# Attention kernel: the transposes of the norm and of the memory's writes in two halves of 64 rows, moved within their slots

## The chip, the cores and the metric

The kernel runs on one core of one Trainium2 chip. The time is the device time of one execution in microseconds (us), read as the median of several runs. The core has a matrix engine (PE; its loading of the stationary operand is listed apart as PEld), a vector engine (DVE), a scalar engine (ACT), a general engine (POOL), and queues that start transfers (SP and others). Each engine works through its own instructions strictly in the order in which they were recorded, and waits on the others by semaphores. Matmuls write to PSUM, which holds eight banks of 128 partitions x 512 float32. ACT and DVE read the results from there.

## The reference, cut to what matters

Four layers, A, B, A, B, each with a layer norm in front and a residual sum behind. A is a linear attention with a learned feature map, B is an attention over four segments of 512 tokens with a memory that is carried from segment to segment:

```python
x = x + A(layernorm(x)); x = x + B(layernorm(x))      # and both once more
# B, 32 heads of 16 columns, N = 4 segments of L = 512 tokens, g = sigmoid(beta) per head
for s in range(N):
    qs, ks, vs = q[:, :, s], k[:, :, s], v[:, :, s]
    p = softmax(qs @ ks.T * Dh**-0.5 + causal_mask)
    a_dot = p @ vs
    a_mem = (phi(qs) @ M) / (phi(qs) @ z + 1e-6)       # phi(t) = t + 1 if t > 0 else exp(t)
    out = g * a_mem + (1 - g) * a_dot
    M, z = M + phi(ks).T @ vs, z + phi(ks).sum()
```

## The kernel before

Everything is float32; products that need the full precision are made of three products of a rounded part and its remainder ("hi" and "lo", hh and hl for the normalised x). The method `steps` of `LayerB` records the attention as one row of **slots**. A segment has eight units m (four groups of eight heads, two halves each), and a unit has five slots, so a slot is named m.j, with 0.0 to 7.4 in each segment. In a slot stand, in this order on PE: the logits of the slot (two matmuls side by side into the tile `lg`, two banks, one buffer), the products from which the row maxima of a later unit are taken ("maxima"), whatever the table names with a leading "<", in slots m.0 the reads of the memory and the weighted sums of the previous unit (`weighted`), and last the quarters of projections that the table names without "<" (Q, V, O).

Four tables (FIRST for the first segment, GAPS for the two in the middle, and LAST and FINAL for the last one of each of the two B layers) say what stands in each slot. The words that matter here: `<t0` to `<t3` transpose the features phi(k) of one group for the memory's write, and `m0` to `m3` are the product and the update that follow; `<ln` is one step of the norm for the next segment, and four of these steps per segment transpose the four 128-token tiles of x (`columns`); `<turn` transposes what the A layer left (in a first segment only), `<max` puts finished maxima into place, `<a0` to `<a3` read the memory. The wrapper `Ordered` and the function `held` keep ACT, DVE, POOL, SP and PE in the order of the recording.

A transpose is a matmul with the identity. `tp` makes one of a block of 128 x 128, with all 128 rows of the array; four of them fill one PSUM tile. Logits, maxima and the projections in the slots use the array in two halves of 64 rows: two matmuls with `tile_position` 0 and 64 run side by side, each into a bank of its own. Reads and `weighted` use column strips instead (128 x 32).

The eight banks are four buffers `g`, two for `lg`, one each for `mx` and `my`. The maxima of a slot take the pair mx, my in slots m.0, m.1 and m.3, and two `g` in m.2 and m.4 (SPARE). A pair of projections holds two `g` for two to four slots. DVE reads each bank of maxima with custom instructions ("tops", each followed by a short READ_ACCUMULATOR). For a write, ACT copies the transposed features from PSUM to the tile KN. For the norm, ACT copies the transposed x to hh and then DVE subtracts, from the same bank, to hl; I call this the subtraction below.

Of the kernel before, what the change touches and what calls it, by code (L numbers as in the profile page):

```python
# [7 lines left out]
F32 = mybir.dt.float32  # L8
# [46 lines left out]


FIRST = """
0.0 <max v3 | 0.1 Q2/6              | 0.2 Q2/6          | 0.3 Q2/6 | 0.4 Q2/6
1.0 <t0 <turn <max m0 | 1.1 fin Q3/6 | 1.2 Q3/6         | 1.3 Q3/6 | 1.4 Q3/6
2.0 <ln <t1 <turn <max m1 | 2.1 fin O/6 | 2.2 O/6       | 2.3 O/6 | 2.4 O/6  # L60
3.0 <ln <turn <turn <max | 3.1 fin O/6 | 3.2 O/6        | 3.3 O/6 | 3.4 O/6
4.0 <ln <ln <max | 4.1 fin Q0+/6    | 4.2 Q0+/6 cv0     | 4.3 Q0+/6 cv1 | 4.4 load Q0+/6
5.0 <t2 <max m2 | 5.1 fin V+/6      | 5.2 V+/6 n        | 5.3 V+/6 n | 5.4 V+/6 w
6.0 <t3 <max m3 | 6.1 fin Q1+/6     | 6.2 Q1+/6 n       | 6.3 Q1+/6 n cv2 | 6.4 Q1+/6 w
7.0 <max <a0+ | 7.1 fin V+/6 w      | 7.2 V+/6 n        | 7.3 V+/6 n | 7.4 V+/6 w
"""
# [35 lines left out]
def interleave_kernel(ctx, tc, x_in, a_wqkv, a_wphi, a_wo, b_wq, b_wk, b_wv, b_wo, b_beta,  # L102
                      c_ident, c_mask, c_bd, out):
    nc = tc.nc
    MUL, ADD, SUB, MAX, MIN = ALU.mult, ALU.add, ALU.subtract, ALU.max, ALU.min
# [17 lines left out]
    def PS(tag, bufs, shape=(P, 512)):  # L123
        return ps.tile(list(shape), F32, tag=tag, bufs=bufs, name=nm(tag))
# [54 lines left out]
    def tp(*a):  # L179
        work[0] += 108  # L180
        return held(nc.tensor.transpose(*a))  # L181
# [831 lines left out]
    class LayerB:  # L1013
# [409 lines left out]
        def steps(self, side, after, table_end):  # L1423
# [3 lines left out]
            N = 8 * NSEG  # L1427
# [6 lines left out]
            outs, turns, proj = {}, {}, {}  # L1434
# [153 lines left out]
    for i in range(2):  # L1588
# [3 lines left out]
        a2 = la[i].pass2()  # L1592
# [40 lines left out]
```

## Time and profile before

| | |
|---|---|
| median of 3 runs | 1307.09 us (1305.85 to 1308.08) |
| the profiled execution | 1307.07 us, span 1305.4 us |
| PE busy | 1266.3 us, 97% of the span |
| DVE busy | 1073.8 us, 82% |
| ACT busy | 835.9 us, 64% |
| POOL busy | 757.8 us, 58% |
| granted PE clock | 0.999 |

The span is that of the instructions in one profiled execution; 1.7 us of its time lie around it. The two B layers' slots lie at about 280 to 660 us and 916 to 1300 us of the span. Rows of a timeline give the start, the duration, the engine, the line, the operation and what it writes and reads, and in brackets how long the engine stood idle before and who released it. A matmul's duration is longer than its share of the engine, since matmuls overlap: the distance of starts is what counts.

### The profile page before, as it was taken

The numbers are of one execution on the slowest core, as the hardware profiler recorded it, in microseconds if no ns is written. First come the engines' busy times: TensorE is split into PE (matmuls) and PEld (weight loads), VectorE is DVE, ScalarE is ACT, GpSimd is POOL, SyncE is SP. The second block draws the span as 40 slices with busy tenths as digits, with TensorE's granted clock in tenths as the row PEclk, the third lists the DMA queues.
The fourth block names the chain that finished last, engine by engine and source line by source line (L and its number), as shares of the span: only waits on it lengthen the run. The fifth ranks groups of instructions, "written<-read, shape, count | busy, mean of one in ns | idle before, by whom it ended". The sixth has DMA issues, their size and how long they took to land.

```text
span 1305.4 us, 41985 instructions
## 1 busy us (share of the span) xinstructions
PE 1266.3 (97%) x16488; PEld 988.1 (76%) x16488; DVE 1073.8 (82%) x3499; ACT 835.9 (64%) x1214; POOL 757.8 (58%) x1124
## 2 busy tenths in 40 slices
PE   7999989999999999999999999999999999999987
PEld 6887868877777777777768887787777777778765
DVE  4776868798998998998867767797899899898995
ACT  5556444648778788777644434455678878877754
POOL 2568855425657768667324346562356766767653
PEclk9999999999999999999999999999999999999999
DMA  6387358545655545545451101855646555554432
GB/s 213 106 314 258 123 175 254 175 125 147 185 164 152 160 126 142 160 134 162 128 174 54 66 34 37 290 176 162 163 127 205 163 141 143 144 142 113 120 84 82
DMA packets 134420, 196.59 MB, mean 151 GB/s; under 512 B 15440, under 2 KB 61648, under 8 KB 133456
## 3 DMA queue, kind: packets, MB, share of 16 engines
q1 hardware_dynamic: 133408, 193.80, 49.1%
q8 instruction: 131, 2.15, 0.7%
q14 instruction: 65, 0.53, 0.1%
q10 hardware_dynamic: 816, 0.11, 0.1%
HBM read 101.05 MB, written 39.85 MB: 108 GB/s over the span
## 4 chain that ended last, share of the span: by engine, by line
PE 77%; DVE 15%; issue 2%; ACT 2%; POOL 2%; DMA 2%; SPq 0%; DVEq 0%; ACTq 0%; POOLq 0%
PE g L177 60%; PE lg L177 6%; PE g L181 4%; PE mx L177 3%; DVE g L155 3%; DVE U L155 2%; PE lg L181 2%; DVE mx L155 2%; DVE my L155 2%; DVE es L155 1%; PE my L177 1%; POOL P L155 1%; DVE mxs L155 1%; ACT P L155 1%; DMA P<-in 1%
## 5 line engine op out<-in xcount | busy, mean ns | idle before, releaser
L155 ACT ACTIVATE P<-lg 128x1024 f32<-128x1024 f32 x316 | 324.1, 1026 | 94.8 <-PE lg L177 75.8
L155 POOL TENSOR_SCALAR_AFFINE_SELECT P<-P 128x256 f32<-128x256 f32 (+1 forms) x448 | 190.0, 442 | 227.4 <-ACT P L155 205.7
L155 DVE CUSTOM_DVE_ANT_0 g<-g,mask 128x128 f32<-128x128 f32 (+3 forms) x392 | 189.4, 538 | 7.0 <-PE g L177 6.7
L155 DVE CUSTOM_DVE_ANT_0 mx<-mx,mask 128x512 f32<-128x512 f32 (+2 forms) x316 | 158.8, 503 | 38.9 <-PE my L177 28.7
L177 PE MATMUL g<-hh,wqk 64*128 64x512 f32 (+1 forms) x960 | 183.2, 393 | 0.7 <-SPq L155 0.4
L177 PE MATMUL g<-w,oh 64*128 64x512 f32 (+2 forms) x848 | 161.8, 380 | 2.6 <-ACT oh L155 2.6
L155 DVE CUSTOM_DVE_ANT_0 my<-my,mask 128x512 f32<-128x512 f32 (+2 forms) x316 | 163.5, 517 | 0.0
L177 PE MATMUL lg<-e,e 64*128 64x512 f32 (+1 forms) x1010 | 145.8, 343 | 7.6 <-ACT P L155 7.5
L177 PE MATMUL g<-P,v 128*32 128x128 f32 (+3 forms) x2064 | 151.7, 433 | 0.2
L177 PE MATMUL g<-w,hh 64*128 64x512 f32 (+1 forms) x672 | 143.5, 395 | 2.4 <-ACT w L155 1.3
L155 DVE DVE_READ_ACCUMULATOR2_ANT mxs<- 128x1 f32 x1024 | 142.9, 140 | 0.0
L177 PEld LDWEIGHTS lg<-e,e 64*128 64x128 f32 x1010 | 92.7, 185 | 51.7 <-ACT P L155 19.7
L177 PEld LDWEIGHTS g<-hh,wqk 64*128 64x128 f32 (+1 forms) x960 | 100.0, 185 | 19.5 <-SPq L155 2.0
L177 PEld LDWEIGHTS g<-P,v 128*32 128x32 f32 x2064 | 65.5, 109 | 60.8 <-issue 53.6
L177 PEld LDWEIGHTS g<-w,oh 64*128 64x128 f32 (+1 forms) x848 | 94.7, 187 | 18.8 <-ACT oh L155 3.5
L155 ACT COPY tb<-g 128x512 f32<-128x512 f32 (+1 forms) x132 | 71.1, 575 | 52.3 <-PE g L177 52.0
L177 PE MATMUL g<-w,ol 64*128 64x512 f32 (+2 forms) x424 | 101.0, 377 | 1.9 <-DVE ol L155 1.9
L177 PE MATMUL g<-hl,wqk 64*128 64x512 f32 (+1 forms) x480 | 102.1, 390 | 0.0
L177 PEld LDWEIGHTS g<-w,hh 64*128 64x128 f32 (+1 forms) x672 | 83.8, 188 | 17.9 <-ACT w L155 1.6
L177 PE MATMUL g<-w,hl 64*128 64x512 f32 (+1 forms) x336 | 89.3, 392 | 0.0
L155 POOL TENSOR_TENSOR ta<-tb,ta 128x512 fp32r<-128x512 f32 x60 | 76.2, 1291 | 14.0 <-ACT ta L155 11.1
L177 PE MATMUL mx<-e,e 63*128 63x256 f32 (+3 forms) x323 | 82.0, 318 | 0.8 <-DVE r L155 0.8
(163 smaller groups left out, 2935.7 us busy)
## 6 DMA issues: line engine op xcount, KB each, us to landing
e<-ta SPq DMA_DIRECT2D x384, 128.0 KB
wqk<-wqk SPq DMA_DIRECT2D x128, 256.0 KB
x<-x SPq DMA_DIRECT2D x48, 256.0 KB
pq<-tb SPq DMA_DIRECT2D x24, 256.0 KB
tb<-pq SPq DMA_DIRECT2D x24, 256.0 KB
x<-xr SPq DMA_DIRECT2D x22, 256.0 KB
xr<-x SPq DMA_DIRECT2D x20, 256.0 KB
x<-in SPq DMA_DIRECT2D x16, 256.0 KB
```

The lines of the kernel that those rows point to most:

```text
L155: i = f(*a, **k)
L177: return held(nc.tensor.matmul(*a, **k))
L181: return held(nc.tensor.transpose(*a))
```

## The change

Three things change, all of them in the B layers' slots only (`banks` is set there and nowhere else).

The new `tp_halves` transposes a block of 128 tokens by 128 columns as two matmuls of 64 rows, with `tile_position` 0 and 64, each into its own bank, 64 columns wide. `columns` and `writes` use it there: four blocks give eight small matmuls in place of four large ones, into two banks in place of one. What was one ACT copy of 512 columns is now two of 256, and the one DVE subtraction of 512 columns is now two of 256.

The new method `pair` chooses the two banks: mx and my in slots m.2 and m.4, where the maxima use `g`, and two buffers `g` in the other slots.

In the tables, the transposes leave the slots m.0. `<t0` to `<t3` go from 1.0, 2.0, 5.0 and 6.0 to 0.4, 1.4, 4.4 and 5.4. The four `<ln` that transpose go from 2.0, 3.0, 4.0 and 4.0 to 2.4, 3.2, 3.3 and 3.4. In a slot m.j with j > 0 they are recorded behind the slot's maxima and ahead of its projections. There are 28 groups of four blocks from `columns` and 24 from `writes` in the slots, 52 in all, spread over seven segments (the last segment of the second B layer has none). The transposes of `<turn`, those of the A layers and those ahead of the slots stay as they were.

```diff
 GAPS = """
-3.0 <ln <turn <turn <max <a2 | 3.1 fin O/6 | 3.2 O/6    | 3.3 O/6 | 3.4 O/6
-4.0 <ln <ln <max <a2 | 4.1 fin Q0+/6 | 4.2 Q0+/6 cv0    | 4.3 Q0+/6 cv1 | 4.4 load begin Q0+/6
+3.0 <turn <turn <max <a2 | 3.1 fin O/6 | 3.2 <ln O/6    | 3.3 <ln O/6 | 3.4 <ln O/6
+4.0  <max <a2 | 4.1 fin Q0+/6 | 4.2 Q0+/6 cv0    | 4.3 Q0+/6 cv1 | 4.4 <t2 load begin Q0+/6
...
+    def tp_halves(outs, in_):
+
+        work[0] += 60
+        for row, out in zip((0, 64), outs):
+            held(nc.tensor.transpose(out, in_[row : row + 64], ident[row : row + 64, row : row + 64],
+                                     tile_position=(row, 0)))
...
+    banks = [None]
+
     def columns(hT, t, x):
+        if banks[0] is not None:
+            pts = [pt[:, 0 : NC * 64] for pt in banks[0]()]
+            for kc in range(NC):
+                tp_halves([pt[:, kc * 64 : (kc + 1) * 64] for pt in pts], x[:, kc * P : (kc + 1) * P])
+            views = [[h[:, :, t * P + 64 * r : t * P + 64 * r + 64] for h in hT]
+                     + [pts[r].rearrange("p (k t) -> p k t", k=NC)] for r in range(2)]
+            for hv, _, pv in views:
+                act.copy(hv, pv)
+            for hv, lv, pv in views:
+                dve.tensor_tensor(out=lv, in0=pv, in1=hv.bitcast(F32), op=SUB)
+            return
         pt = PS("g", G)
...
             ph = self.st[s, c]["phi", 1]
-            pt = PS("g", G)
+            pts = [pt[:, 0 : 4 * 64] for pt in self.pair()]
             for t in range(4):
-                tp(pt[:, t * P : (t + 1) * P], ph[:, t * P : (t + 1) * P], ident)
+                tp_halves([pt[:, t * 64 : (t + 1) * 64] for pt in pts], ph[:, t * P : (t + 1) * P])
             pk = T2("KN", 1)
-            act.copy(pk, pt)
+            for r in range(2):
+                act.copy(pk.rearrange("p (t r f) -> p r t f", t=4, r=2)[:, r],
+                         pts[r].rearrange("p (t f) -> p t f", t=4))
...
+        def pair(self):
+
+            return [PS(t, 1) for t in ("mx", "my")] if self.k % R in SPARE else [PS("g", G) for _ in range(2)]
...
+                banks[0] = self.pair if 0 <= k < R * N else None
```

**PE, slot 4.0 of the third segment of the first B layer.** Before, from the logits (lg) over the maxima (mx, my) to the memory's reads (mem). x are tiles of normalised tokens, w and oh or ol a projection's operands.

```order
L177 MATMUL g_8325<-w_4999,ol_7641 128x512
L177 MATMUL lg_8438<-e_433_2751,e_434_2752 128x512 x2
L177 MATMUL mx_8442<-e_453_2833,e_452_2832 128x256
L177 MATMUL my_8443<-e_453_2833,e_452_2832 128x256
L177 MATMUL mx_8442<-e_453_2833,e_452_2832 128x384
L177 MATMUL my_8443<-e_453_2833,e_452_2832 128x384
L181 MATMUL g_8452<-ident,x_6675 128x128 x4
L181 MATMUL g_8459<-ident,x_6677 128x128 x4
L177 MATMUL g_8471<-mem_2746,tb_1298_7678 32x34 x32
```

And the same place in the changed kernel:

```order
L177 MATMUL g_8441<-w_5058,ol_7745 128x512
L177 MATMUL lg_8596<-e_433_2751,e_434_2752 128x512 x2
L177 MATMUL mx_8600<-e_453_2833,e_452_2832 128x256
L177 MATMUL my_8601<-e_453_2833,e_452_2832 128x256
L177 MATMUL mx_8600<-e_453_2833,e_452_2832 128x384
L177 MATMUL my_8601<-e_453_2833,e_452_2832 128x384
L177 MATMUL g_8615<-mem_2746,tb_1317_7795 32x34 x32
```

The two groups of transposes between the maxima and the reads are gone from this slot; one went to slot 3.3 and one to 3.4.

**PE, slot 3.2 of the same segment, the changed kernel**, from the maxima (here in two `g`) to the first matmul of the projection O (pair w, oh):

```order
L177 MATMUL g_8464<-e_434_2752,e_433_2751 128x384
L177 MATMUL g_8465<-e_434_2752,e_433_2751 128x384
L187 MATMUL mx_8477<-ident,x_6778 128x64
L187 MATMUL my_8478<-ident,x_6778 128x64
L187 MATMUL mx_8477<-ident,x_6778 128x64
L187 MATMUL my_8478<-ident,x_6778 128x64
L187 MATMUL mx_8477<-ident,x_6778 128x64
L187 MATMUL my_8478<-ident,x_6778 128x64
L187 MATMUL mx_8477<-ident,x_6778 128x64
L187 MATMUL my_8478<-ident,x_6778 128x64
L177 MATMUL g_8441<-w_5058,oh_6699 128x512
```

Before, the projection followed the maxima directly; the eight half transposes now stand between them and write mx and my, which the maxima of slot 3.3 write next.

**DVE, slots 3.2 and 3.3 there.** Before, from the last top of slot 3.2 (g) through the four of slot 3.3 (mx, my) to the first of slot 3.4 (ISA are a top and its READ_ACCUMULATOR, mxs the maxima):

```order
L155 ISA g_8349,mxs_2748<-g_8349,mask 128x384
L155 ISA mxs_2748 128x1
L155 ISA mx_8382,mxs_2748<-mx_8382,mask 128x256
L155 ISA mxs_2748 128x1
L155 ISA my_8383,mxs_2748<-my_8383,mask 128x256
L155 ISA mxs_2748 128x1
L155 ISA mx_8382,mxs_2748<-mx_8382,mask 128x256
L155 ISA mxs_2748 128x1
L155 ISA my_8383,mxs_2748<-my_8383,mask 128x256
L155 ISA mxs_2748 128x1
L155 ISA g_8414,mxs_2748<-g_8414,mask 128x512
```

And in the changed kernel, from the same top on:

```order
L155 ISA g_8465,mxs_2748<-g_8465,mask 128x384
L155 ISA mxs_2748 128x1
L155 TENSOR_TENSOR hl_8303<-mx_8477,hh_8302 128x4x64
L155 TENSOR_TENSOR hl_8303<-my_8478,hh_8302 128x4x64
L155 ISA mx_8512,mxs_2748<-mx_8512,mask 128x256
L155 ISA mxs_2748 128x1
L155 ISA my_8513,mxs_2748<-my_8513,mask 128x256
L155 ISA mxs_2748 128x1
L155 ISA mx_8512,mxs_2748<-mx_8512,mask 128x256
L155 ISA mxs_2748 128x1
L155 ISA my_8513,mxs_2748<-my_8513,mask 128x256
L155 ISA mxs_2748 128x1
```

Two subtractions of half the width now stand ahead of the tops of slot 3.3 (two more follow those, and two follow the tops of 3.4); before, DVE had none from 3.1 to 3.4, and two of the full width in 4.0.

More of the change, by code (lines that the diff above doesn't have):

```diff
@@ L57 @@
 FIRST = """
[L58 to L64, printed above, removed]
+0.0 <max v3 | 0.1 Q2/6              | 0.2 Q2/6          | 0.3 Q2/6 | 0.4 <t0 Q2/6
+1.0 <turn <max m0 | 1.1 fin Q3/6 | 1.2 Q3/6         | 1.3 Q3/6 | 1.4 <t1 Q3/6
+2.0 <turn <max m1 | 2.1 fin O/6 | 2.2 O/6       | 2.3 O/6 | 2.4 <ln O/6
+3.0 <turn <turn <max | 3.1 fin O/6 | 3.2 <ln O/6        | 3.3 <ln O/6 | 3.4 <ln O/6
+4.0  <max | 4.1 fin Q0+/6    | 4.2 Q0+/6 cv0     | 4.3 Q0+/6 cv1 | 4.4 <t2 load Q0+/6
+5.0 <max m2 | 5.1 fin V+/6      | 5.2 V+/6 n        | 5.3 V+/6 n | 5.4 <t3 V+/6 w
+6.0 <max m3 | 6.1 fin Q1+/6     | 6.2 Q1+/6 n       | 6.3 Q1+/6 n cv2 | 6.4 Q1+/6 w
 7.0 <max <a0+ | 7.1 fin V+/6 w      | 7.2 V+/6 n        | 7.3 V+/6 n | 7.4 V+/6 w
@@ L67 @@
 GAPS = """
-0.0 <max <a0 n | 0.1 fin Q2/6 n     | 0.2 Q2/6 n        | 0.3 Q2/6 n cv3 | 0.4 Q2/6
-1.0 <t0 <turn <max <a1 m0 | 1.1 fin Q3/6 | 1.2 Q3/6     | 1.3 Q3/6 | 1.4 Q3/6
-2.0 <ln <t1 <turn <max <a1 m1 | 2.1 fin O/6 | 2.2 O/6   | 2.3 O/6 | 2.4 O/6
-3.0 <ln <turn <turn <max <a2 | 3.1 fin O/6 | 3.2 O/6    | 3.3 O/6 | 3.4 O/6
-4.0 <ln <ln <max <a2 | 4.1 fin Q0+/6 | 4.2 Q0+/6 cv0    | 4.3 Q0+/6 cv1 | 4.4 load begin Q0+/6
-5.0 <t2 <max <a3 m2 | 5.1 fin V+/6 | 5.2 V+/6 n N       | 5.3 V+/6 n N | 5.4 V+/6
-6.0 <t3 <max <a3 m3 | 6.1 fin Q1+/6 | 6.2 Q1+/6 n N     | 6.3 Q1+/6 n N cv2 | 6.4 Q1+/6
+0.0 <max <a0 n | 0.1 fin Q2/6 n     | 0.2 Q2/6 n        | 0.3 Q2/6 n cv3 | 0.4 <t0 Q2/6
+1.0 <turn <max <a1 m0 | 1.1 fin Q3/6 | 1.2 Q3/6     | 1.3 Q3/6 | 1.4 <t1 Q3/6
+2.0 <turn <max <a1 m1 | 2.1 fin O/6 | 2.2 O/6   | 2.3 O/6 | 2.4 <ln O/6
+3.0 <turn <turn <max <a2 | 3.1 fin O/6 | 3.2 <ln O/6    | 3.3 <ln O/6 | 3.4 <ln O/6
+4.0  <max <a2 | 4.1 fin Q0+/6 | 4.2 Q0+/6 cv0    | 4.3 Q0+/6 cv1 | 4.4 <t2 load begin Q0+/6
+5.0 <max <a3 m2 | 5.1 fin V+/6 | 5.2 V+/6 n N       | 5.3 V+/6 n N | 5.4 <t3 V+/6
+6.0 <max <a3 m3 | 6.1 fin Q1+/6 | 6.2 Q1+/6 n N     | 6.3 Q1+/6 n N cv2 | 6.4 Q1+/6
 7.0 <max <a0+ | 7.1 fin V+/6      | 7.2 V+/6 n N        | 7.3 V+/6 n N | 7.4 V+/6
@@ L79 @@
 1.0 <turn <max <a1 | 1.1 fin Q3/6   | 1.2 Q3/6          | 1.3 Q3/6 | 1.4 Q3/6
-2.0 <ln <turn <max <a1 | 2.1 fin O/6 | 2.2 O/6          | 2.3 O/6 | 2.4 O/6
-3.0 <ln <turn <turn <max <a2 | 3.1 fin O/6 | 3.2 O/6    | 3.3 O/6 | 3.4 O/6
-4.0 <ln <ln <max <a2 | 4.1 fin v/2  | 4.2 v/2 cv0       | 4.3 v/2 cv1 | 4.4 v/2
+2.0 <turn <max <a1 | 2.1 fin O/6 | 2.2 O/6          | 2.3 O/6 | 2.4 <ln O/6
+3.0 <turn <turn <max <a2 | 3.1 fin O/6 | 3.2 <ln O/6    | 3.3 <ln O/6 | 3.4 <ln O/6
+4.0  <max <a2 | 4.1 fin v/2  | 4.2 v/2 cv0       | 4.3 v/2 cv1 | 4.4 v/2
 5.0 <max <a3 | 5.1 fin v/2          | 5.2 v/2           | 5.3 v/2 | 5.4 v/2
@@ L1554, in steps @@
                         do(w, s, k)
-            put_off[0] = None
+            put_off[0], banks[0] = None, None
             for f in self.late + self.rows:
```

## The prediction

> **What bounds the kernel now.** I read the page first, then busy time by windows, then the chain of waits inside the slots, then timelines of PE and DVE at each place where a transpose leaves or arrives.
>
> ```profile
> span 1305.4 us, 41985 instructions
> PE 1266.3 (97%) x16488; PEld 988.1 (76%) x16488; DVE 1073.8 (82%) x3499; ACT 835.9 (64%) x1214; POOL 757.8 (58%) x1124
> PE 77%; DVE 15%; issue 2%; ACT 2%; POOL 2%; DMA 2%; SPq 0%; DVEq 0%; ACTq 0%; POOLq 0%
> ```
>
> PE carries 77% of the chain, DVE 15%. For the unit from slot 3.1 to 4.1 of the third segment (first B layer) the window gives, after the window and its length, PE, PEld and DVE busy:
>
> ```profile
> 515.79:528.13 12.34, 12.34 (x188) 9.69 (x185) 11.34 (x44) 7.76 (x10) 6.29 (x10) 1.00 0.40 110
> ```
>
> DVE is busy 11.34 of 12.34 us. So in the slots two engines are nearly full, and the chain confirms it; in the unit after this one it lies on DVE for 8 us, from here to the next row of PE:
>
> ```profile
> 528.92 0.69 DVE mx L155
> ...
> 536.77 0.66 PE g L181 x4
> ```
>
> Within a unit DVE falls behind PE from m.1 to m.4, where tops come fast, and catches up in m.0, where PE spends most of its time on `weighted`. The change takes work off PE in m.0 and puts work on DVE, and two banks, into m.2 to m.4. That is where I expect its price.
>
> **What is removed from PE.** Timeline of PE: the last pair of maxima, then transposes, then the reads of the memory: slot 3.0 with one group, slot 4.0 with two, and a slot without any.
>
> ```profile
> 512.03 0.34 PE L177 MATMUL mx<-e,e 63*128 63x384 f32 x1
> ...
> 512.89 0.77 PE L177 MATMUL g<-mem,tb 128*32 128x34 f32 x64
> ```
> ```profile
> 523.91 0.34 PE L177 MATMUL mx<-e,e 63*128 63x384 f32 x1
> ...
> 524.18 1.09 PE L181 MATMUL g<-ident,x 128*128 128x128 f32 x8
> 525.20 0.77 PE L177 MATMUL g<-mem,tb 128*32 128x34 f32 x64
> ```
> ```profile
> 572.59 0.33 PE L177 MATMUL my<-e,e 63*128 63x384 f32 x1
> 572.86 0.77 PE L177 MATMUL g<-mem,tb 128*32 128x34 f32 x64
> ```
>
> Starts lie 0.86, 1.29 and 0.27 us apart. So one group alone costs 0.86 - 0.27 = 0.59 us, two cost 1.02, the second 0.43. The first includes the step into the full array and out again. In a first segment, slots 1.0 to 3.0 keep `<turn` transposes, and there each group saves only 0.43.
>
> Per middle segment: four single slots (1.0, 3.0, 5.0, 6.0) and two with two groups (2.0, 4.0), 4 x 0.59 + 2 x 1.02 = 4.4 us; per first segment about 3.9; in the last segment of the first layer (2.0, 3.0, 4.0) 2.2. All: 4 x 4.4 + 2 x 3.9 + 2.2 = 27.6 us.
>
> **What is added to PE.** 52 groups of four pairs of half transposes. No row shows one.
>
> ```profile
> L181 PE MATMUL g<-ident,x 128*128 128x128 f32 x256 | 38.0, 277 | 1.1 <-ACT x L155 1.1
> ...
> L181 PEld LDWEIGHTS g<-ident,x 128*128 128x128 f32 x256 | 29.5, 140 | 9.6 <-issue 3.1 <-ACT x L155 1.3 <-DVE mxs L155 1.0
> ```
> ```profile
> L177 PEld LDWEIGHTS mx<-e,e 63*128 63x128 f32 x316 | 57.0, 186 | 8.8 <-issue 2.4 <-DVE r L155 1.3 <-DVE mxs L155 0.7
> ```
>
> A full transpose takes 0.43 / 4 = 0.11 us. If the two halves of a pair run side by side, as 64-row matmuls do (mx and my below start 0.01 apart), and half the moving columns take half the time, a pair costs 0.06, a group 0.24. If the pair is as slow as a full block, 0.11 and 0.43. Below 0.24 I see no row, and nothing negative is possible for instructions that must issue. I take 0.24, because loading for a transpose lasts 140 ns against 186 for other matmuls, which says that the load is not what fills the 0.11. Sum 52 x 0.24 = 12.5 us. PE alone would therefore gain 27.6 - 12.5 = 15.1 us. No full-array step is added: neighbours in m.1 to m.4 use 64 rows already.
>
> **What is added to DVE and ACT.**
>
> ```profile
> L155 DVE TENSOR_TENSOR hl<-g,hh 128x512 fp32r<-128x512 f32 x48 | 32.1, 686 | 8.6 <-ACT hh L155 8.4
> ...
> L155 DVE TENSOR_TENSOR ot<-g,r 128x256 f32<-128x256 f32 x64 | 27.2, 425 | 2.2
> ```
> ```profile
> L155 ACT COPY tb<-g x132: 358/587/630, 46.4 to 1274.5; 128x512 f32<-128x512 f32 x124, 128x256 f32<-128x256 f32 x8
> ```
>
> A half subtraction lasts 0.42 us (the nearest row, also from PSUM); DVE rows below start about 0.08 before the previous ends, so two take 0.35 + 0.42. The copies take 0.36 each (the shortest of the row) in place of 0.59. ACT is busy 64% and I charge it nothing by itself: exp ends about 1.1 us after the transposes arrive and copies follow while PE does 1.4 us of projection. Without that cover the cost is 0.1 per group. What counts is when the banks come free.
>
> **The cluster 3.2 to 4.0.** PE, before:
>
> ```profile
> 518.35 0.63 PE L177 MATMUL g<-w,oh 64*128 64x512 f32 x4
> ...
> 520.03 0.28 PE L177 MATMUL my<-e,e 63*128 63x256 f32 x1
> ...
> 520.27 0.64 PE L177 MATMUL g<-w,oh 64*128 64x512 f32 x4
> ...
> 521.91 0.41 PE L177 MATMUL g<-e,e 63*128 63x512 f32 x2
> 522.15 0.64 PE L177 MATMUL g<-w,oh 64*128 64x512 f32 x4
> ...
> 523.80 0.28 PE L177 MATMUL my<-e,e 63*128 63x256 f32 x1
> ```
>
> and DVE:
>
> ```profile
> 520.44 0.59 DVE L155 CUSTOM_DVE_ANT_0 g<-g,mask 128x384 f32<-128x384 f32 x1
> ...
> 520.95 0.46 DVE L155 CUSTOM_DVE_ANT_0 mx<-mx,mask 128x256 f32<-128x256 f32 x1
> ...
> 522.10 0.46 DVE L155 CUSTOM_DVE_ANT_0 my<-my,mask 128x256 f32<-128x256 f32 x1
> ...
> 523.13 0.73 DVE L155 CUSTOM_DVE_ANT_0 g<-g,mask 128x512 f32<-128x512 f32 x1
> ```
>
> DVE runs without a gap here and starts the mx top 0.92 us after PE wrote mx. From a DVE end to a waiting PE start I allow 0.1 us.
> (1) Slot 3.2: transposes at 518.35 find mx, my free, +0.24. The subtractions run behind the g tops, 520.95 to 521.73. The maxima of 3.3 need my, free at 521.83 in place of 520.03: everything queued behind them on PE (transposes, O, the next logits) is late by 521.83 - 520.03, less the little that mx gains: +1.78.
> (2) Slot 3.3: four tops (0.38 apart) now end their turn at 523.33, two subtractions on `g` follow, end 524.1, free 524.2. O holds two of the four `g`, so the maxima of 3.4 must have these: 524.2 for 521.91, +2.29.
> (3) Slot 3.4: transposes, projection and logits, PE at 4.0 at 526.3. DVE: two tops of 0.65 from about 524.35, then two subtractions, my free at 526.5 against 523.80: +2.7.
> 4.0 is then 1.02 shorter: **net +1.7 us**. What is late next is `weighted`, and with it all of the next unit.
>
> **The other sites.** Transposes at m.4 in mx, my wait for the tops of m.3. For 2.4 (DVE, then PE):
>
> ```profile
> 510.01 0.46 DVE L155 CUSTOM_DVE_ANT_0 my<-my,mask 128x256 f32<-128x256 f32 x1
> ...
> 511.10 0.73 DVE L155 CUSTOM_DVE_ANT_0 g<-g,mask 128x512 f32<-128x512 f32 x1
> ```
> ```profile
> 510.29 0.64 PE L177 MATMUL g<-w,oh 64*128 64x512 f32 x4
> ...
> 511.92 0.28 PE L177 MATMUL my<-e,e 63*128 63x256 f32 x1
> ```
>
> Wait 510.47 + 0.1 - 510.29 = 0.28, transposes 0.24, then subtractions behind the g tops free my at 512.62 while PE is there at 512.44: +0.2. Less 0.59 in 3.0: **+0.13**. For 4.4:
>
> ```profile
> 534.99 0.46 DVE L155 CUSTOM_DVE_ANT_0 my<-my,mask 128x256 f32<-128x256 f32 x1
> ```
> ```profile
> 534.47 0.40 PE L177 MATMUL g<-hh,wqk 64*128 64x512 f32 x2
> ...
> 536.08 0.28 PE L177 MATMUL mx<-e,e 63*128 63x256 f32 x1
> ...
> 537.41 0.36 PE L177 MATMUL g<-mem,tb 128*32 128x34 f32 x20
> ```
>
> Wait 535.45 + 0.1 - 534.47 = 1.08, +0.24, +0.1 for the KN copies. In 5.0 the transposes waited for DVE anyway: 1.33 from maxima to reads becomes 0.38, -0.95. **+0.47**. Read in the same way: 0.4 waits 0.33, net -0.02; 1.4 waits 0.17, net 0.17 + 0.24 - 1.02 = -0.61; 5.4 waits 0.31, net -0.04. Over the 24 sites of writes the wait goes from none to 1.15; the last of them, 0.29:
>
> ```profile
> 1181.93 0.47 DVE L155 CUSTOM_DVE_ANT_0 my<-my,mask 128x256 f32<-128x256 f32 x1
> ```
> ```profile
> 1182.21 0.64 PE L177 MATMUL g<-w,hh 64*128 64x512 f32 x4
> ```
>
> Sum of this segment: -0.02 - 0.61 + 0.13 + 1.7 + 0.47 - 0.04 = +1.6. The other middle ones, with shorter waits, give +0.9, +1.35, +1.5; the first ones, saving less, +1.9 and +1.8; the last, where DVE lags less, +1.5. Total **+10.6 us**: 1307.07 + 10.6 = 1317.7, and as the profiled execution equals the median of 1307.09, that is the forecast.
>
> **Rivals.**
> *Faster: DVE is not late.* In m.0 DVE loses up to 1.2 us of subtractions. If that head start lasted to m.3, banks would be free when PE comes. The seven clusters would then each be 3 x 0.24 - 1.02 = -0.3 in place of +1.7, 14 us less: 1304; without any wait at the other sites either, 1307.1 - 15.1 = 1292. I take 1300 between them. It decides once the delay at 4.0 falls under 1.2 instead of 2.7 (seven times 1.5 is the 10.6). Against it: DVE goes idle before the tops of m.1 today (528.92 follows PE's 0.43 of logits), so a head start is lost there. Chance 0.22.
> *No change.* Half of the cluster's delay is absorbed: 1305 to 1309. Chance 0.13.
> *Slower still: the pair is load-bound.* 0.11 per pair, 0.2 more at the 30 sites outside the clusters and 0.2 per cluster: +7.4, 1325. Chance 0.13. The Trainium skill, "TensorE: Matmul & The Clock Gate", section LDWEIGHTS, has the load cost its columns over 1.2 GHz whatever the rows, an estimate of 0.43 per group here. The 140 against 186 ns for equal columns speaks against it; a half transpose the trace of before does not hold.
> *The halves don't run side by side.* 0.87 per group, +0.63 over my sum at 30 sites, 0.9 in seven clusters: 1343. Chance 0.04; 64-row pairs do overlap today.
>
> **How the numbers follow.** Forecast 0.48, its own range 1310 to 1322. A measurement here tells 0.2% (2.6 us) from no change. Faster 0.22, same 0.13, slower 0.48 + 0.13 + 0.04 = 0.65. Range 1301 to 1325: it takes in the lower edge of the faster case's middle and the load-bound pair, and leaves out the rest of the faster case and the serial halves.
>
> **What would show it.** Right: in 3.3, 3.4 and 4.0 PE idle before mx, my, g, released by DVE's hl subtraction; before the transposes of 4.4 an idle of 1 us, released by tops; the unit 3.1 to 4.1 near 14.0 us for 12.34; a group of pairs near 0.24. Wrong: PE starting 4.0's maxima within 1.2 us of the old distance from 3.1; pairs 0.11 apart; DVE idle between 3.1 and 3.4.

## The result and the profile after

| | before | changed |
|---|---|---|
| median of 4 runs | 1306.47 us (1304.52 to 1308.08) | 1319.92 us (1319.25 to 1320.84) |
| span of the profiled execution | 1305.4 us | 1319.1 us |

The changed kernel takes 1.0104 times as long, with a 95% interval of 1.0087 to 1.0122. It is slower by about 13.4 us.

The head of the page of the changed kernel and its busy times:

```profile
span 1319.1 us, 42457 instructions
PE 1270.0 (96%) x16696; PEld 993.3 (75%) x16696; DVE 1077.4 (82%) x3527; ACT 838.2 (64%) x1266; POOL 757.6 (57%) x1124
```

PE is busy for 3.7 us more and DVE for 3.6 us more. The span grew by 13.7 us, so most of it is waiting. The waits of PE name what is new: none of these three rows stands among the waits of the kernel before (L187 is the line of the half transposes).

```profile
PE mx L177 <- DVE hl L155: 6.3, 7, 1.0
PE mx L187 <- DVE mxs L155: 3.4, 6, 0.6
PE mx L177 <- DVE ot L155: 1.0, 1, 1.0
```

(The columns are: total us, number of waits, longest one.) The seven waits on hl are one per segment. The window over the unit 3.1 to 4.1 of the third segment of the first B layer, the one the prediction works through, has these columns: the window and its length, then PE, PEld and DVE busy:

```profile
518.35:532.64 14.29, 13.39 (x205) 10.45 (x202) 12.27 (x49) 8.41 (x14) 6.26 (x10) 1.00 0.35 95
```

The unit takes 14.29 us in place of 12.34. The timeline of PE in it, from slot 3.2 on:

```profile
520.90 0.22 PE L187 MATMUL my<-ident,x 64*128 64x64 f32 x1
520.91 0.22 PE L187 MATMUL mx<-ident,x 64*128 64x64 f32 x1
520.96 0.22 PE L187 MATMUL my<-ident,x 64*128 64x64 f32 x1
...
521.11 0.72 PE L177 MATMUL g<-w,oh 64*128 64x512 f32 x4
...
523.96 0.38 PE L177 MATMUL mx<-e,e 63*128 63x256 f32 x1 [0.90 <-DVE hl L155]
524.29 0.38 PE L177 MATMUL my<-e,e 63*128 63x256 f32 x1
...
526.69 0.83 PE L177 MATMUL g<-e,e 63*128 63x512 f32 x2
...
529.10 0.28 PE L177 MATMUL mx<-e,e 63*128 63x256 f32 x1
529.29 0.38 PE L177 MATMUL my<-e,e 63*128 63x256 f32 x1
```

and of DVE:

```profile
523.49 0.41 DVE L155 TENSOR_TENSOR hl<-mx,hh 128x256 fp32r<-128x256 f32 x1
523.83 0.41 DVE L155 TENSOR_TENSOR hl<-my,hh 128x256 fp32r<-128x256 f32 x1
524.72 0.43 DVE L155 CUSTOM_DVE_ANT_0 mx<-mx,mask 128x256 f32<-128x256 f32 x1 [0.48 <-PE mx L177]
...
526.21 0.76 DVE L155 TENSOR_TENSOR hl<-g,hh 128x256 fp32r<-128x256 f32 x2
527.22 0.70 DVE L155 CUSTOM_DVE_ANT_0 g<-g,mask 128x512 f32<-128x512 f32 x1 [0.26 <-PE g L177]
...
528.82 0.42 DVE L155 TENSOR_TENSOR hl<-my,hh 128x256 fp32r<-128x256 f32 x1
529.77 0.30 DVE L155 CUSTOM_DVE_ANT_0 mx<-mx,mask 128x128 f32<-128x128 f32 x1 [0.53 <-PE mx L177]
```

The pairs of half transposes start 0.06 us apart and the two of a pair within 0.01. PE then waits in three slots for a bank that a subtraction still reads. In 3.3 it stands still for 0.90 us: mx starts at 523.96, when the subtraction of mx has just ended (523.49 + 0.41 = 523.90), and my 0.33 later, when that of my has. In 3.4 and 4.0 the profile shows no idle time, since earlier matmuls still run, but the starts tell the wait. The two maxima of 3.4 start 0.33 us apart, each as a subtraction on `g` ends; before, they started 0.02 apart. In 4.0 my starts 0.19 behind mx, at 529.29, when the subtraction of my has ended (528.82 + 0.42 = 529.24). DVE stands still in its turn, for 0.48 us in 3.3, 0.26 in 3.4 and 0.53 in 4.0, until PE has filled the next bank. Before, DVE ran through 3.2 to 3.4 without a gap, and its one wait here was 0.36 us in 4.0:

```profile
524.28 0.30 DVE L155 CUSTOM_DVE_ANT_0 mx<-mx,mask 128x128 f32<-128x128 f32 x1 [0.36 <-PE my L177]
```

So in this stretch each of the two engines waits for the other.

The same matmul can be found in both traces by its place in the order, so that its start in the one less its start in the other is the **delay** at that point. Summed over the seven segments, and between one profiled execution of each kernel, the sites of the change add: 0.4 with 1.0, -0.7 us; 1.4 with 2.0, -3.6; 2.4 with 3.0, +1.2; the cluster 3.2 to 4.0, **+13.9** (1.76 to 2.13 in each segment); 4.4 with 5.0, +3.0; 5.4 with 6.0, -0.2. That is +13.6 in all. The cluster alone is as large as the whole difference.

### The profile page after: what moved, and what is told of

It is laid out like the page before. It is cut to its first block, busy times and chain, and to the rows that moved or that the text cites. A ratio compares the mean times of both kernels' runs of the same rounds, so it can differ in the third digit from the quotient of the medians.

```text
span 1319.1 us, 42457 instructions
## 1 busy us (share of the span) xinstructions
PE 1270.0 (96%) x16696; PEld 993.3 (75%) x16696; DVE 1077.4 (82%) x3527; ACT 838.2 (64%) x1266; POOL 757.6 (57%) x1124
## 5 line engine op out<-in xcount | busy, mean ns | idle before, releaser
L177 PE MATMUL g<-hh,wqk 64*128 64x512 f32 (+1 forms) x960 | 186.6, 395 | 0.7 <-DMA wqk<-wqk 0.3
L177 PE MATMUL g<-w,oh 64*128 64x512 f32 (+2 forms) x848 | 168.1, 385 | 3.0 <-ACT oh L155 2.6
L177 PE MATMUL lg<-e,e 64*128 64x512 f32 (+1 forms) x1010 | 149.1, 342 | 7.6 <-ACT P L155 7.5
L177 PE MATMUL g<-P,v 128*32 128x128 f32 (+3 forms) x2064 | 151.8, 433 | 0.0
L177 PE MATMUL g<-w,hh 64*128 64x512 f32 (+1 forms) x672 | 143.8, 395 | 2.7 <-ACT w L155 1.3
L155 DVE DVE_READ_ACCUMULATOR2_ANT mxs<- 128x1 f32 x1024 | 145.7, 142 | 0.1
L177 PEld LDWEIGHTS lg<-e,e 64*128 64x128 f32 x1010 | 96.5, 184 | 49.7 <-ACT P L155 19.2
L177 PEld LDWEIGHTS g<-hh,wqk 64*128 64x128 f32 (+1 forms) x960 | 102.8, 185 | 17.8 <-SPq L155 1.4
L177 PEld LDWEIGHTS g<-w,oh 64*128 64x128 f32 (+1 forms) x848 | 98.9, 187 | 17.4 <-ACT oh L155 3.5
L177 PEld LDWEIGHTS g<-P,v 128*32 128x32 f32 x2064 | 65.3, 109 | 60.8 <-issue 51.8
L177 PE MATMUL g<-w,ol 64*128 64x512 f32 (+2 forms) x424 | 105.8, 377 | 1.9 <-DVE ol L155 1.9
L177 PE MATMUL g<-hl,wqk 64*128 64x512 f32 (+1 forms) x480 | 103.5, 390 | 0.0
L177 PEld LDWEIGHTS g<-w,hh 64*128 64x128 f32 (+1 forms) x672 | 83.6, 187 | 18.0 <-ACT w L155 1.6
L177 PE MATMUL mx<-e,e 63*128 63x256 f32 (+3 forms) x323 | 85.7, 325 | 7.3 <-DVE hl L155 6.3
L177 PE MATMUL g<-w,hl 64*128 64x512 f32 (+1 forms) x336 | 89.5, 391 | 0.0
L177 PE MATMUL g<-e,e 63*128 63x256 f32 (+3 forms) x488 | 85.3, 353 | 0.1
```

The lines of the kernel that those rows point to most:

```text
L155: i = f(*a, **k)
L177: return held(nc.tensor.matmul(*a, **k))
```

## The experiments

Two readings were open. **The hold:** the price is banks that DVE keeps from PE. **The work:** the price is the larger number of smaller instructions, wherever they stand. All ratios below are against the kernel before, run on the same chip, with 95% intervals. The site sums of all of them are in one table behind the experiments.

### Halves in the old slots

```diff
 GAPS = """
-0.0 <max <a0 n | 0.1 fin Q2/6 n     | 0.2 Q2/6 n        | 0.3 Q2/6 n cv3 | 0.4 <t0 Q2/6
-1.0 <turn <max <a1 m0 | 1.1 fin Q3/6 | 1.2 Q3/6     | 1.3 Q3/6 | 1.4 <t1 Q3/6
+0.0 <max <a0 n | 0.1 fin Q2/6 n     | 0.2 Q2/6 n        | 0.3 Q2/6 n cv3 | 0.4 Q2/6
+1.0 <t0 <turn <max <a1 m0 | 1.1 fin Q3/6 | 1.2 Q3/6     | 1.3 Q3/6 | 1.4 Q3/6
...
```

> The half transposes, their two banks and their smaller copies and subtractions stay; the four tables are those of before, so that the transposes stand in m.0 again, there in two g buffers. Theory (the price is banks that DVE holds in m.2 to m.4, the cluster 3.2 to 4.0 above all): without the move the price is gone and what is left is the gain of a group, 0.43 - 0.24 = 0.19 us and some of the 0.16 for the step into the full array and out, against a wait in 2.0 and 4.0, where the second group needs four g while a pair of projections holds two. About -5 us against before: 1297 to 1306. Rival (the smaller instructions themselves cost: 28 more subtractions of 0.1 us on DVE, 52 more copies on ACT, 208 more matmuls, wherever they stand): slower than before by about as much as the change is, 1315 to 1322.

Measured: 1320.36 us, ratio 1.0100 (1.0082 to 1.0117). The theory expected a gain of 5 us and was off by some 17; the number is the rival's. The waits of PE in its profile tell why:

```profile
PE g L177 <- DVE hl L155: 8.5, 9, 1.2
...
PE g L187 <- DVE mxs L155: 3.3, 11, 0.4
```

The timeline of PE in its slot 4.0, third segment, and then in its slot 5.0:

```profile
527.91 0.58 PE L187 MATMUL g<-ident,x 64*128 64x64 f32 x9
528.70 0.46 PE L187 MATMUL g<-ident,x 64*128 64x64 f32 x7 [0.21 <-ACT tb L155]
530.08 0.77 PE L177 MATMUL g<-mem,tb 128*32 128x34 f32 x64 [0.92 <-DVE hl L155]
```

```profile
541.63 0.27 PE L187 MATMUL g<-ident,tb 64*128 64x64 f32 x1 [0.24 <-DVE mxs L155]
542.27 0.46 PE L187 MATMUL g<-ident,tb 64*128 64x64 f32 x7 [0.38 <-DVE mxs L155]
```

In 4.0 two groups of halves take all four `g`, and the reads of the memory, which need a `g`, wait 0.92 us for a subtraction. In 5.0 the first half finds its bank after 0.24 us, as the full transposes did before; the second needs a second bank, in which DVE is still looking for maxima, and waits 0.38 us more. So m.0 was no free place for halves: a group in two banks needs **two** banks to be free, and DVE holds `g` there too. The mechanism is the same. My expectation named the wait of the second group in 2.0 and 4.0 without giving it a size, and left out that of a single group.

### Only the writes moved, only the columns moved

```diff
-2.0 <turn <max <a1 m1 | 2.1 fin O/6 | 2.2 O/6   | 2.3 O/6 | 2.4 <ln O/6
-3.0 <turn <turn <max <a2 | 3.1 fin O/6 | 3.2 <ln O/6    | 3.3 <ln O/6 | 3.4 <ln O/6
-4.0  <max <a2 | 4.1 fin Q0+/6 | 4.2 Q0+/6 cv0    | 4.3 Q0+/6 cv1 | 4.4 <t2 load begin Q0+/6
+2.0 <ln <turn <max <a1 m1 | 2.1 fin O/6 | 2.2 O/6   | 2.3 O/6 | 2.4 O/6
+3.0 <ln <turn <turn <max <a2 | 3.1 fin O/6 | 3.2 O/6    | 3.3 O/6 | 3.4 O/6
+4.0 <ln <ln <max <a2 | 4.1 fin Q0+/6 | 4.2 Q0+/6 cv0    | 4.3 Q0+/6 cv1 | 4.4 <t2 load begin Q0+/6
```

> The changed kernel with only the writes (t0 to t3) in their new slots; the norm's four transposes go back to 2.0, 3.0, 4.0 and 4.0, as halves, in two g. Theory: the cluster's 14 us (2.0 in each of seven segments) go, and the writes' sites keep what they show in the change's trace (about -0.5 us in sum); 2.0 and 3.0 gain about 0.35 each, 4.0 loses by a wait for g: 1299 to 1307. Rival (the instructions cost, not the place): 1315 to 1322.

Measured: 1315.62 us, ratio 1.0061 (1.0046 to 1.0076): a miss by 9 us, on the rival's lower edge. The cluster's 13.9 us fell only to 7.9, since the two groups in 4.0 are halves and wait for `g` as in the run above (+1.0 to +1.4 per segment).

The other half of the table, with `<t0` to `<t3` back in 1.0, 2.0, 5.0 and 6.0 and the `<ln` left in 2.4, 3.2, 3.3 and 3.4:

```diff
-1.0 <turn <max <a1 m0 | 1.1 fin Q3/6 | 1.2 Q3/6     | 1.3 Q3/6 | 1.4 <t1 Q3/6
-2.0 <turn <max <a1 m1 | 2.1 fin O/6 | 2.2 O/6   | 2.3 O/6 | 2.4 <ln O/6
+1.0 <t0 <turn <max <a1 m0 | 1.1 fin Q3/6 | 1.2 Q3/6     | 1.3 Q3/6 | 1.4 Q3/6
+2.0 <t1 <turn <max <a1 m1 | 2.1 fin O/6 | 2.2 O/6   | 2.3 O/6 | 2.4 <ln O/6
...
```

> The changed kernel with only the norm's transposes in their new slots (2.4, 3.2, 3.3, 3.4); t0 to t3 go back to 1.0, 2.0, 5.0 and 6.0, as halves, in two g. Theory: the cluster keeps its price of about 2.0 us in each of seven segments and 2.4 its 0.16, +15 us; the writes alone in their m.0 gain about 0.35 each at 24 sites, -8: 1311 to 1318, above e3 by 10 us or more. Rival (the instructions cost): the same as the change, 1317 to 1322, and e3 as well.

Measured: 1319.60 us, ratio 1.0095 (1.0078 to 1.0112), above the expected range by 1.6 us and inside the rival's. The cluster is at +13.9 as expected; that the writes would gain 8 us in m.0 did not come true except in 2.0 (-5.2), where one group is left in place of two. By the medians the two runs differ by 4 us only, not by 10, because each still contains a place where halves wait for a second bank. These three runs alone would allow either reading; the next two do not.

### Who frees the bank: ACT alone, with POOL or with DVE behind it

```diff
-            for hv, _, pv in views:
-                act.copy(hv, pv)
-            for hv, lv, pv in views:
-                dve.tensor_tensor(out=lv, in0=pv, in1=hv.bitcast(F32), op=SUB)
+            xv = x.rearrange("p (k r t) -> p r k t", k=NC, r=2)
+            for r in range(2):
+                act.copy(xv[:, r], views[r][2])
+            hv, lv = [h[:, :, t * P : (t + 1) * P] for h in hT]
+            xk = x.rearrange("p (k t) -> p k t", k=NC)
+            act.copy(hv, xk)
+            pool.tensor_tensor(out=lv, in0=xk, in1=hv.bitcast(F32), op=SUB)
```

> The changed kernel, slots and halves as they are, but in the slots ACT copies both halves unrounded from PSUM back into x (two copies of 256 columns), then makes hh from x, and POOL makes hl from x and hh in SBUF. So the two banks come free after ACT alone, about 1 us earlier in the cluster, and DVE has 0.77 us less per group; ACT has one copy of 512 more. Theory (banks held by DVE's queue): the cluster's +2.0 us per segment falls to about +0.2, the rest stays: 1306, 1303 to 1311. Rival (the number of instructions or the place on PE costs, not the banks): no gain, since there are more instructions still: 1318 to 1325.

Measured: 1310.52 us, ratio 1.0023 (1.0011 to 1.0035), against 1319.92 for the change: inside the expected range, near its upper end. The slots hold 28 copies on ACT and 28 subtractions on POOL more, and 56 half subtractions on DVE fewer, so that there are as many instructions as in the change. The cluster costs 0.55 to 0.63 us in six segments, where +0.2 was expected, and 2.17 in the last one of the first layer, 5.6 in all in place of 13.9, and the row of waits on hl is gone. But this also took work off DVE, so the same edit was run with the last line on DVE:

```diff
-            pool.tensor_tensor(out=lv, in0=xk, in1=hv.bitcast(F32), op=SUB)
+            dve.tensor_tensor(out=lv, in0=xk, in1=hv.bitcast(F32), op=SUB)
```

> As the run in which POOL subtracts, but with the subtraction on DVE again, now from x and hh in SBUF: ACT alone frees the two banks, while DVE has its subtraction of 512 columns (about 0.7 us) in every group, as much work as in the change. It parts two readings of the cluster: DVE holds the banks, or DVE has too much to do. Theory (the hold): the cluster costs +0.5 to +1.0 per segment in place of 2.0, 1309 to 1314 in all. Rival (DVE's work): the cluster stays near 2.0 and the whole near the change, 1317 to 1323.

Measured: 1311.94 us, ratio 1.0019 (1.0007 to 1.0031). DVE is busy for as long as in the change (1078.0 us against 1077.4), its 28 subtractions from SBUF take even longer than the 56 halves from PSUM did (23.9 us against 22.8), yet the cluster is at 5.4:

```profile
PE 1264.5 (97%) x16696; PEld 994.4 (76%) x16696; DVE 1078.0 (82%) x3499; ACT 854.2 (65%) x1294; POOL 761.9 (58%) x1124
```

```profile
L155 DVE TENSOR_TENSOR hl<-x,hh 128x512 fp32r<-128x512 f32 x28 | 23.9, 854 | 7.2 <-ACT hh L155 7.2
```

So it is not DVE's amount of work that costs 8 us in the cluster, but that this work stood between PE and its bank. Nor does less of it gain anything that can be seen: with POOL, DVE is busy for 18.7 us less, and the two runs lie 2.6 and 2.7 us above the kernel before. What the bank still costs there is the wait of the transposes themselves in 3.3, for the second `g` that a top holds (first half, second half):

```profile
521.51 0.27 PE L187 MATMUL g<-ident,x 64*128 64x64 f32 x1
522.03 0.28 PE L187 MATMUL g<-ident,x 64*128 64x64 f32 x2 [0.24 <-DVE mxs L155]
```

The last segment of the first layer keeps most of its price (1.45 us here and 2.17 with POOL, 1.75 in the change) by a wait of another kind. A projection of PE waits there for SP; in the run with POOL:

```profile
615.77 0.73 PE L177 MATMUL g<-w,oh 64*128 64x512 f32 x4 [0.44 <-SPq L155]
621.72 0.73 PE L177 MATMUL g<-w,oh 64*128 64x512 f32 x4 [1.35 <-SPq L155]
```

and SP's queue in that stretch issues weights of an A layer (awv):

```profile
617.70 2.34 SPq L155 DMA_DIRECT2D w<-awv  x2
```

With DVE one such wait is left, of 1.01 us; before and the change have none in this cluster. Less these waits the segment costs 0.38 and 0.44, no more than the others do. Why SP comes late there no run tests.

### Full blocks in the new slots

```diff
-            pts = [pt[:, 0 : NC * 64] for pt in banks[0]()]
-            for kc in range(NC):
-                tp_halves([pt[:, kc * 64 : (kc + 1) * 64] for pt in pts], x[:, kc * P : (kc + 1) * P])
+        pt = banks[0]() if banks[0] is not None else PS("g", G)
+        for kc in range(NC):
+            tp(pt[:, kc * P : (kc + 1) * P], x[:, kc * P : (kc + 1) * P], ident)
...
-            return [PS(t, 1) for t in ("mx", "my")] if self.k % R in SPARE else [PS("g", G) for _ in range(2)]
+            return PS("mx", 1) if self.k % R in SPARE else PS("g", G)
```

> The changed kernel's tables, but blocks transposed with all 128 rows into one bank (mx in m.2 and m.4, one g elsewhere), one copy and one subtraction of 512 columns, as before. It parts the halves from the place. Theory: the cluster still waits for the subtraction in mx (0.69 in place of 0.77, hardly less), and each group is 0.19 dearer on PE and steps into the full array and out (0.16): +0.35 at 28 sites outside the clusters and about +0.3 per group in the clusters, less where the one bank comes free sooner than two: 1322 to 1336, slower than the change by 3 to 16. Rival (two banks and small instructions are the price, wherever they stand): the place alone gains, 1300 to 1312.

Measured: 1328.86 us, ratio 1.0172 (1.0156 to 1.0188), as the theory expected. Halves and place have no price each by itself. Against the kernel before, full blocks in the new slots cost 21.6 us, halves in the new slots 13.4, and halves in the old slots 12.4. Halving takes back 8 us in the new slots and costs 12 in the old ones, where a group needs two of the four `g` at once. The timeline of PE around a full block between 64-row neighbours:

```profile
523.43 0.46 PE L177 MATMUL g<-e,e 63*128 63x256 f32 x4
523.83 0.66 PE L181 MATMUL mx<-ident,x 128*128 128x128 f32 x4
524.41 0.74 PE L177 MATMUL g<-w,oh 64*128 64x512 f32 x4
```

From the block's start to the next projection's lie 0.58 us, where the halves take 521.11 - 520.90 = 0.21.

Both halves into one bank, which would have answered the shortage directly, was not tried. The Trainium skill, "TensorEngine Tiling (Array Packing)", section Gotcha 1: PSUM Pressure, states that different row tiles cannot use one bank at the same time, and that row tiling therefore asks for more PSUM; no run here shows the first. The second agrees: the waits for a further `g` above, 0.38 and 0.92 us, are its price in this case.

### Chosen places

```diff
 GAPS = """
-1.0 <t0 <turn <max <a1 m0 | 1.1 fin Q3/6 | 1.2 Q3/6     | 1.3 Q3/6 | 1.4 Q3/6
-2.0 <ln <t1 <turn <max <a1 m1 | 2.1 fin O/6 | 2.2 O/6   | 2.3 O/6 | 2.4 O/6
-3.0 <ln <turn <turn <max <a2 | 3.1 fin O/6 | 3.2 O/6    | 3.3 O/6 | 3.4 O/6
-4.0 <ln <ln <max <a2 | 4.1 fin Q0+/6 | 4.2 Q0+/6 cv0    | 4.3 Q0+/6 cv1 | 4.4 load begin Q0+/6
+1.0 <turn <max <a1 m0 | 1.1 fin Q3/6 | 1.2 Q3/6     | 1.3 Q3/6 | 1.4 Q3/6
+2.0 <t1 <turn <max <a1 m1 | 2.1 fin O/6 | 2.2 O/6   | 2.3 O/6 | 2.4 <ln O/6
+3.0 <ln <turn <turn <max <a2 | 3.1 fin O/6 | 3.2 <ln O/6    | 3.3 O/6 | 3.4 O/6
+4.0 <ln <max <a2 | 4.1 fin Q0+/6 | 4.2 Q0+/6 cv0    | 4.3 Q0+/6 cv1 | 4.4 load begin Q0+/6
...
+        def halves(self):
+
+            m, j, s = self.slot
+            return self.pair() if j or m == 2 or m == 3 and s else None
```

(Against the kernel before; `<t0` is in 0.4. Where `halves` gives None, a full block goes into one `g`, as before; in slots m.j with j > 0 POOL makes hl from SBUF.)

> Halves only where a pair of banks is free by what the runs so far show: t0 in 0.4, t1 in 2.0, the norm's transposes in 2.4, 3.0 (halves there in middle and last segments, a full block in first ones) and 3.2, and the fourth of them as a full block in one g in 4.0; t2 and t3 as full blocks in one g in 5.0 and 6.0, as before. In 2.4 and 3.2 POOL makes hl from SBUF, as in the experiment before. Theory (a second bank is the price wherever DVE still holds it, and two groups in one slot m.0 are what can be saved): t0 -0.9 in sum, 2.0 -5.2, 2.4 and 3.0 -0.5, cluster 7 x (0.31 - 0.43) = -0.8, the rest as before: -7 against before, 1297 to 1304. Rival (more instructions cost by their number wherever they stand): between before and the run with POOL, 1307 to 1311.

Measured: 1308.77 us, ratio 1.0017 (1.0004 to 1.0030), 5 us above the expected range and inside the rival's. The sites tell the two apart: t0 gives -0.6 (-0.9 expected), 2.0 gives -4.5 (-5.2), and six of the seven clusters -0.16 to -0.09 each (-0.12), which a price by number would not give. Two sites are what it lacks: 2.4 and 3.0 together cost +2.9 where -0.5 was expected (a group in 2.4 adds 0.58 in the third segment, and 3.0 gives back only 0.27), and the cluster of the last segment of the first layer costs +1.74, of which 0.65 is again a wait for SP and 0.68 one of the logits of 4.0 for an ACT copy. Leaving out both gives the last run; in it the group of 2.4 is back in 4.0, and the last segment of the first layer has its four groups in 2.0, 3.0, 4.0 and 4.0 again:

```diff
-2.0 <t1 <turn <max <a1 m1 | 2.1 fin O/6 | 2.2 O/6   | 2.3 O/6 | 2.4 <ln O/6
+2.0 <t1 <turn <max <a1 m1 | 2.1 fin O/6 | 2.2 O/6   | 2.3 O/6 | 2.4 O/6
...
-4.0 <ln <max <a2 | 4.1 fin Q0+/6 | 4.2 Q0+/6 cv0    | 4.3 Q0+/6 cv1 | 4.4 load begin Q0+/6
+4.0 <ln <ln <max <a2 | 4.1 fin Q0+/6 | 4.2 Q0+/6 cv0    | 4.3 Q0+/6 cv1 | 4.4 load begin Q0+/6
```

> Only the moves that showed a gain or a small price: t0 as halves in 0.4; t1 as halves alone in 2.0; the norm's transposes in 3.0 (halves in two g in middle segments, a full block in first ones), 3.2 (halves, with POOL's subtraction) and twice in 4.0 (full blocks); the last segment of the first layer has its four in 2.0, 3.0, 4.0 and 4.0, t2 and t3 stay full in 5.0 and 6.0. By the sites measured so far: t0 -0.6, 2.0 -4.5, 3.0 -0.8, 3.2 six times +0.31, the rest nothing: about -4 us, 1300 to 1305, just more than can be told from no change. Rival (what one site gains is taken back at the next wait on DVE): within 0.2% of before, 1305 to 1310.

Measured: **1304.14 us**, ratio 0.9961 (0.9947 to 0.9975): faster than before by 0.4%, and than the change by 1.4% if the two ratios are compared. It lies inside the expected range, and 5.1 us below before where about 4 was expected. PE in its slot 4.0, where the full blocks stand as before, and the reads behind them do not wait:

```profile
523.76 1.09 PE L181 MATMUL g<-ident,x 128*128 128x128 f32 x8
524.78 0.77 PE L177 MATMUL g<-mem,tb 128*32 128x34 f32 x64
```

Here are the site sums of all kernels, in us against the kernel before, over seven segments, each from the start of the same matmul in one profiled execution of each kernel (so that a tenth or two is not to be read), and below them the difference of the medians:

| site | change | old slots | writes only | columns only | POOL | DVE from SBUF | full blocks | chosen | fewer |
|---|---|---|---|---|---|---|---|---|---|
| 0.4, 1.0 | -0.7 | -0.6 | -1.0 | -0.4 | -0.9 | -1.1 | +0.3 | -0.6 | -0.9 |
| 1.4, 2.0 | -3.6 | +3.4 | -1.8 | -5.2 | -3.5 | -3.5 | -2.2 | -4.5 | -4.4 |
| 2.4, 3.0 | +1.2 | +0.2 | +0.4 | +1.3 | +0.5 | +0.5 | +1.5 | +2.9 | -1.2 |
| 3.2 to 4.0 | +13.9 | +8.1 | +7.9 | +13.9 | +5.6 | +5.4 | +16.3 | +1.0 | +1.9 |
| 4.4, 5.0 | +3.0 | +2.1 | +3.7 | +2.4 | +3.8 | +3.3 | +2.6 | +0.1 | +0.7 |
| 5.4, 6.0 | -0.2 | -0.1 | -0.4 | -0.2 | -0.2 | -0.3 | +1.2 | +0.1 | 0.0 |
| sum | +13.6 | +13.0 | +8.8 | +11.8 | +5.3 | +4.3 | +19.7 | -1.0 | -3.9 |
| medians | +13.4 | +12.4 | +7.7 | +11.6 | +2.6 | +2.7 | +21.6 | +1.5 | -5.1 |

The two last rows agree within 3 us throughout.

## Why the prediction was right

The forecast of 1317.7 us was 2.2 us low. As a difference from before, +10.6 us was forecast and +13.4 measured. The sign, the place and the mechanism were right: the price is banks that DVE's subtractions hold, in the cluster above all.

- **The half transposes.** 0.06 us per pair and 0.21 to 0.24 per group, as taken. The rivals by which a pair is bound by its load, or its halves run one behind the other, are refuted. The load of a half lasts 139 ns, against 140 for a full block, and yet pairs follow at twice the rate of full blocks. The Trainium skill, "TensorE: Matmul & The Clock Gate", section LDWEIGHTS, has a load cost its columns over 1.2 GHz whatever the rows, an estimate of 0.107 us for 128. That the rows don't count agrees with the equal durations, though these are 0.14 us, longer than the estimate; the 0.11 us from one full block to the next agrees with its size. The 0.06 us per pair does not, so that for row halves it is no bound on the rate here.

```profile
L187 PEld LDWEIGHTS mx<-ident,x x84: 134/139/142, 315.9 to 1169.4; 64*128 64x128 f32 x84
L187 PE MATMUL mx<-ident,x x84: 216/222/275, 316.0 to 1169.4; 64*128 64x64 f32 x84
```

- **The half subtractions.** Two were to take 0.35 + 0.42 and take 0.34 + 0.41 (523.49, 523.83, above).
- **The cluster.** The first delay was put at 1.78 and is 524.29 - 520.03 less the 2.56 by which slot 3.1 started later, 1.70. The second was put at 2.29 and is 526.69 - 521.91 - 2.56 = 2.22. The third was put at 2.7 and is 529.29 - 523.80 - 2.56 = 2.93. This is the term that was mis-sized: I let the tops of 3.3 follow the subtractions at once, at about 521.73; they began at 524.72 - 2.56 = 522.16, since DVE waited 0.48 us for PE to fill mx. The tops of 3.4 so began at 527.22 - 2.56 = 524.66 in place of 524.35. (The wait of 0.26 ahead of these was in the sum, between 524.1 and 524.35.) Less the 1.02 saved in 4.0 (measured 0.98) that is +1.95 in place of +1.7. All seven clusters cost 13.9, where seven times 1.7 would be 11.9.
- **The other sites of that segment.** 2.4 with 3.0: +0.11 (predicted +0.13). 1.4 with 2.0: -0.64 (-0.61). 4.4 with 5.0: +0.52 (+0.47). 0.4 with 1.0: +0.17 (-0.02). 5.4 with 6.0: +0.05 (-0.04). With the cluster the segment costs 2.2 where 1.6 was predicted. The other segments in the middle and the first ones are low by about as much (1.3, 1.8 and 2.1 against 0.9, 1.35 and 1.5; 2.5 and 2.7 against 1.9 and 1.8), and the last was put too high (1.0 against 1.5).

Of what the prediction names as signs of being right, the unit 3.1 to 4.1 takes 14.29 us where it says near 14.0, and the idle time of PE ahead of a held bank shows as such only in 3.3. One of its signs of being wrong came true as well: "DVE idle between 3.1 and 3.4" is the 0.48 and 0.26 us above. It was meant for a DVE that is in time. Here DVE is idle because PE, held by DVE's own subtraction, has not yet filled the next bank, so the sign could not tell the two cases apart. And outside the clusters stand 31 groups (24 of writes, 7 in 2.4), where the rivals counted 30 and the expectation for the full blocks 28; this moves their times by 1 us at most.

The wait ahead of the transposes of 4.4 stands as predicted. From the start of the maxima to the first half lie 0.96 us and to the second 1.34; less the 0.24 that a pair of maxima takes, that is a wait of 0.72 for the top of mx and of 1.10 for that of my, where 1.08 was predicted:

```profile
538.71 0.39 PE L177 MATMUL g<-e,e 63*128 63x512 f32 x2
539.67 0.27 PE L187 MATMUL mx<-ident,tb 64*128 64x64 f32 x1 [0.57 <-DVE mxs L155]
540.05 0.27 PE L187 MATMUL my<-ident,tb 64*128 64x64 f32 x1
```

The two profiled executions differ by 12.0 us at the last logits, a little less than the sites, and by 13.7 in the span: 1.7 us lie behind the last matmul. Between the B layers, at about 810 us, 1.1 to 1.2 us come back, in all the kernels run; the trace of before has a wait of 1.3 us there for which it shows no releaser ("PE my L177 <- issue: 1.3, 1, 1.3" in the waits of that stretch), and the changed kernel's has none. Why PE paused there is open, and so is what the end adds. That the sum of the sites and the difference of the medians agree to 0.2 us is therefore in part luck.

What I saw only with the experiments is that the halves' second bank is scarce in m.0 as well. The prediction's rival "faster" looked for a gain in DVE being in time; the gain that there was (0.4%) lay mostly in taking one of two groups out of 2.0 (-4.4), and less in the halves that had two banks in 3.0 and in 0.4 (-1.2 and -0.9).

## What to carry to other kernels

Before a transpose (or any PSUM producer) is moved under a cover on PE, ask who empties its bank and what stands ahead of that on the emptying engine's queue: the bank is free only then, and everything behind it on PE waits. If the emptier is the engine that is already behind, let another one copy the bank out first, even at the cost of one more copy per group; that took 8 of 14 us back here. Splitting over row tiles doubles the number of banks that must be free at once, so split only where two are. Whether it pays depends on the place: here it gained 8 us in the new slots and lost 12 in the old ones.

## What was not expected of the hardware

- Half transposes of 64 rows reach one pair per 0.06 us with loads of 139 ns each, where full ones follow at 0.11 with loads of 140.
- On DVE a subtraction of 512 columns lasted 0.85 us on average with both operands in SBUF, and 0.69 with one in PSUM (the first row below is of the same run). On POOL, from SBUF, it lasted 1.29 us (the second):

```profile
L155 DVE TENSOR_TENSOR hl<-g,hh 128x512 fp32r<-128x512 f32 x20 | 13.5, 688 | 8.6 <-ACT hh L155 8.4
```

```profile
L155 POOL TENSOR_TENSOR hl<-x,hh 128x512 fp32r<-128x512 f32 x28 | 36.2, 1294 | 1.6 <-ACT hh L155 1.3 <-DMA w<-awv 0.3
```
